# Retention and two MLP layers on one core: sums of the right operands on VectorE, weight preparation outside one block, a fourth w_out buffer

## Chip, cores and metric

The kernel runs on one core of a Trainium2 chip. The metric is the device time in microseconds, the median of three runs; a profiled execution of the same program stands beside them.

## What is computed

```python
# q, k, v: (4, 8, 576, 64); x is then (2304, 512); w_in (512, 2048), w_out (2048, 512), twice
scores = (q @ k.T) / sqrt(64) * gamma_h ** (i - j)   # for i >= j, else 0
x = (scores @ v), heads side by side                 # 2304 tokens x 512
h = x @ w_in;  x = (max(h, 0) ** 2) @ w_out          # layer one
h = x @ w_in2; out = (h * clip(h + 3, 0, 6) / 6) @ w_out2   # layer two
```

The weights arrive as 8-byte floats and all products are to have the accuracy of 4-byte floats. The kernel decodes the weights itself and splits each factor into a high part (what the matmul's input type holds) and a low part (the rest); a product is three matmuls: high by high, high by low, low by high.

## The kernel before

**Layer one** goes over five blocks of tokens (`FIRST`, line 26: 512, 512, 512, 256, 512) and in each over 16 chunks of the 2048 hidden columns. One chunk of one block is a unit; there are 80, numbered from 0, and the block of 256 is units 48 to 63. A unit i issues, in this order: the 12 matmuls of h (`emit_h`, line 348); in the last three units of a block the high and low parts of the next block's x (`split_x`); the parts of the w_in chunk of unit i + 1 (`split_in`, high on ScalarE, low on VectorE from unit 17 on); in units 1 to 16 the parts of a w_out chunk (`split_out`); relu on ScalarE, square, and the parts of g (`emit_g`); pieces of the retention of later tokens; the 12 matmuls of y for unit i - 2 (`y_steps`, `LAG` = 2); the load of the w_out parts of unit i + 1 (`load_out`); and preparation steps. The first block decodes layer one's weights as it goes and stores the w_out parts to memory (`keep`), from where later blocks load them. The w_out tiles rotate through the pool `wop` of three buffers; in units 15 and 16 the last two tiles made by `split_out` and the first reloads alternate in it.

**Preparation** (`ready_steps`, line 414) makes the weights of layer two: eight groups of 11 steps, in the order decode, decode, sums (GpSimd), split, decode, split, w_out split, split, decode, split, w_out split. A decode has two ScalarE and four VectorE operations and a load of the next staged weight; a split has its high part on ScalarE and its low part on GpSimd, a w_out split its low part on VectorE; each ends in a store. They stand at the end of units 16 to 73, `READY` (line 46), at 88/58 = 1.5 steps a unit, issued when a whole step is owed.

**Layer two** uses the seven products of a Strassen scheme (`PRODUCTS`, line 48: P1 P6 P2 P7 P5 P4 P3) on three blocks of 768 tokens (`SECOND`), two halves of 384 each. A pair (`pair`, line 533) is two chunks of hidden columns in one block: seven products of six matmuls, and between the products, in slots 0 to 6 (`between`), the y matmuls of the pair before and side work. There are 24 pairs, eight a block. The left operands come from memory (`load_left`), the right operands are made once a block from x by `operand_steps` (line 461): four sums on GpSimd (768 columns in one operation, line 468) and seven splits (`split_to`, lines 174 and 175: high part on ScalarE, low part on VectorE, 768 columns each). For the first block this is done in the last units of layer one and slots 0, 2 and 4 of the first pair; for a later block in slots 0, 2, 4 and 5 of the last pair of the block before and slots 0, 2 and 4 of its own first pair. Each operand lies in the place that the same product's operand of the block before had, so it can't be made before that is used up.

Each engine works its instructions in the order of the program, and the order is written by hand. The SP queue issues nearly all DMAs, also in order: a transfer that waits holds back those behind it.

Of the kernel before, what the change touches and what calls it, by code (L numbers as in the profile page):

```python
# [9 lines left out]
F32 = mybir.dt.float32  # L10
# [4 lines left out]
ALU = mybir.AluOpType  # L15
# [29 lines left out]

READY = (16, 74)

# [18 lines left out]
def retention_moe_moe2(ctx, tc, qk, qk_last, kv, w_in, w_out, w_in2, w_out2, consts, out):  # L66
# [16 lines left out]
    one = pool("one", 1)  # L83
    wop = pool("wo", 3)
    cp = pool("cp", 3)
    banks = pool("banks", 1, space=PSUM)
# [14 lines left out]
    def place(tag, shape, dtype, name):  # L101


        return one.tile(shape, dtype, tag=tag, name=name)
# [356 lines left out]
    def operand_steps(j):  # L461

        t0 = SECOND[j]
        b = lambda k, t: xall[:, 2 * k:2 * k + 2, t0 + HALF * t:t0 + HALF * t + HALF]
        tt = {}

        def minus(dst, x, y):
            nc.gpsimd.tensor_tensor(out=dst, in0=x, in1=y, op=ALU.subtract)  # L468

        def step(i):  # L470
            name = PRODUCTS[i]
            if name == "P6":
                tt[2] = place("ret", [128, 2, 512], F32, "t2")[:, :, :HALF]
                minus(tt[2], b(1, 1), b(0, 0))
            if name == "P7":
                minus(b(0, 1), b(1, 1), b(0, 1))
            src = {
                "P1": b(0, 0), "P6": tt.get(2), "P2": b(1, 0), "P7": b(0, 1), "P5": b(0, 0),
                "P4": b(1, 0), "P3": b(1, 1),
            }[name]  # L480
            if i < 3:
                t = place(f"x{i + 4}", [128, 2, 2, HALF], F32R, "xop")
            else:
                t = place(f"x{i - 3}", [128, 2, 2, HALF], F32R, "xop")
            split_to(t[:, 0], t[:, 1], src, nc.vector)
            operands[j, name] = t
            if name == "P1":
                minus(b(0, 0), b(0, 1), b(0, 0))
            if name == "P2":
                minus(b(1, 0), b(1, 0), tt[2])  # L490

        return [lambda i=i: step(i) for i in range(len(PRODUCTS))]

# [136 lines left out]
    with tc.manual_schedule():  # L630
# [39 lines left out]
        ready = [f for p in range(NPAIR) for f in ready_steps(p)]  # L670
        pace, owed = len(ready) / (READY[1] - READY[0]), 0
        following = operand_steps(0)
        for i, (pos, c) in enumerate(units):
# [55 lines left out]
        following.pop(0)()  # L729
        load_left(1)  # L730
# [5 lines left out]
        for k in range(total):  # L736
# [69 lines left out]
```

## Time and profile before

| | |
|---|---|
| median of 3 runs | 933.23 us (931.39 to 933.29) |
| profiled execution | 932.34 us, span 930.4 us |
| TensorE matmuls busy | 876.8 us (94%) |
| VectorE / ScalarE / GpSimd busy | 594.2 / 424.0 / 190.9 us |
| mean granted TensorE clock | 0.978 |
| mean memory traffic | 207 GB/s |

A busy share is an average over stages; what sets the time of one stage is read from the waits of TensorE in it. In the rows PE is TensorE's matmul, PEld its weight load, which runs ahead of the matmul, DVE is VectorE, ACT ScalarE, POOL GpSimd, SP SyncE (SPq its queue of DMA issues). L175 is line 175 of the kernel before.

### The profile page before, as it was taken

How to read it: one execution, taken by the hardware profiler on the slowest of the kernel's cores; microseconds unless marked ns; L12 is line 12 of the kernel's file. 1: busy time of each engine (PE TensorE's matmuls, PEld its weight loads, DVE VectorE, ACT ScalarE, POOL GpSimd, SP SyncE). 2: the span in 40 equal slices, each digit the busy share in tenths (PEclk: the TensorE clock that was granted, in tenths of full speed). 3: DMA queues.
4: the chain of work that ended last, by engine and by line, in shares of the span. 5: the costliest groups of instructions: out<-in, count | busy, mean ns of one | idle time of the engine just before them, and what ended most of it. 6: DMA issues, size and time to landing. Idle time of an engine off the chain costs nothing.

```text
span 930.4 us, 13279 instructions
## 1 busy us (share of the span) xinstructions
PE 876.8 (94%) x4986; PEld 743.5 (80%) x4986; DVE 594.2 (64%) x933; ACT 424.0 (46%) x777; POOL 190.9 (21%) x157
## 2 busy tenths in 40 slices
PE   8788989899999999987999999999799998999998
PEld 6666766677888888876888888898688896888896
DVE  5699987777686768878765653535644346544443
ACT  2466675534554355545553443334343333433332
POOL 4455533323122313242131200002100003000000
PEclk8899999899999999998999999999899999999999
DMA  9357776675676676977747554545175554375432
GB/s 351 112 182 254 226 258 210 210 260 206 198 238 223 223 260 218 312 247 273 248 134 235 217 190 156 210 163 205 67 294 194 179 186 164 114 279 195 171 124 90
DMA packets 72879, 192.56 MB, mean 207 GB/s; under 512 B 10480, under 2 KB 26864, under 8 KB 72816
## 3 DMA queue, kind: packets, MB, share of 16 engines
q1 hardware_dynamic: 72672, 191.39, 59.9%
q8 instruction: 39, 0.64, 0.3%
q10 hardware_dynamic: 144, 0.34, 0.1%
q14 instruction: 24, 0.20, 0.1%
HBM read 155.53 MB, written 36.18 MB: 206 GB/s over the span
## 4 chain that ended last, share of the span: by engine, by line
PE 69%; DVE 13%; ACT 8%; DMA 4%; issue 4%; POOL 1%; SPq 0%; DVEq 0%; ACTq 0%; POOLq 0%
PE yps L517 19%; PE hps L547 17%; PE yps L388 15%; PE hps L354 15%; DMA stage<-in_w_in_dram 4%; DVE a L154 2%; DVE a L163 2%; DVE wd L169 1%; ACT a L152 1%; DVE ret L238 1%; DVE a L157 1%; PE vps L277 1%; DVE xop L175 1%; DVE win L175 1%; ACT xop L174 1%
## 5 line engine op out<-in xcount | busy, mean ns | idle before, releaser
L354 PE MATMUL hps<-xring,win 128*128 128x512 f32 (+1 forms) x960 | 220.7, 377 | 24.9 <-DVE win L175 12.5
L517 PE MATMUL yps<-wo,g 128*128 128x512 f32 x864 | 228.7, 396 | 8.7 <-ACT g L560 4.7
L388 PE MATMUL yps<-g,wo 128*128 128x512 f32 (+1 forms) x960 | 218.1, 375 | 1.9 <-POOL wo L175 1.2
L354 PEld LDWEIGHTS hps<-xring,win 128*128 128x128 f32 x960 | 169.3, 192 | 62.6 <-DVE win L175 14.9
L547 PE MATMUL hps<-xop,win 128*128 128x384 f32 x1008 | 206.8, 339 | 2.9 <-DVE xop L175 1.7
L547 PEld LDWEIGHTS hps<-xop,win 128*128 128x128 f32 x1008 | 182.8, 190 | 20.0 <-DVE xop L175 2.4
L388 PEld LDWEIGHTS yps<-g,wo 128*128 128x128 f32 x960 | 169.3, 192 | 35.0 <-POOL wo L175 2.0
L517 PEld LDWEIGHTS yps<-wo,g 128*128 128x128 f32 x864 | 160.8, 189 | 33.6 <-ACT g L560 5.3
L174 ACT ACTIVATE g<-r 128x512 fp32r<-128x512 f32 (+1 forms) x80 | 47.2, 590 | 101.7 <-DVE r L371 101.1
L566 DVE TENSOR_TENSOR u<-hps,u 128x384 f32<-128x384 f32 x48 | 26.8, 557 | 96.1 <-PE hps L547 96.1
L175 DVE TENSOR_TENSOR g<-r,g 128x512 fp32r<-128x512 f32 (+1 forms) x80 | 57.0, 713 | 42.2 <-ACT g L174 40.7
L367 ACT ACTIVATE r<-hps 128x512 f32<-128x512 f32 (+1 forms) x80 | 44.0, 550 | 75.8 <-PE hps L354 75.7
L560 ACT ACTIVATE g<-c 128x384 fp32r<-128x384 f32 x72 | 37.8, 525 | 88.1 <-DVE c L559 86.6
L371 DVE TENSOR_TENSOR r<-r 128x512 f32<-128x512 f32 (+1 forms) x64 | 47.8, 747 | 34.1 <-ACT r L367 34.1
L468 POOL TENSOR_TENSOR xall<-xall 128x768 f32<-128x768 f32 x6 | 12.0, 2006 | 249.1 <-DVE xop L175 249.1
L558 ACT ACTIVATE v<-c,three 128x384 f32<-128x384 f32 x72 | 44.4, 617 | 38.8 <-DVE c L566 37.9
L175 DVE TENSOR_TENSOR win<-w,win 128x512 fp32r<-128x512 f32 x63 | 52.1, 827 | 3.2 <-ACT win L174 3.2
L154 DVE TENSOR_SCALAR a<-a 128x512 f32<-128x512 f32 x64 | 43.5, 680 | 15.1 <-ACT a L152 14.9
L559 DVE SCALAR_TENSOR_TENSOR c<-v,c 128x384 f32<-128x384 f32 x72 | 43.2, 600 | 12.9 <-ACT v L558 12.9
L174 ACT ACTIVATE win<-w 128x512 fp32r<-128x512 f32 x80 | 49.5, 619 | 0.0
L585 ACT ACTIVATE c<-hps 128x384 f32<-128x384 f32 x24 | 11.8, 492 | 82.7 <-PE hps L547 82.7
L152 ACT ACTIVATE a<-stage 128x512 f32<-128x512 f32 x64 | 42.2, 660 | 13.0 <-DMA stage<-in_w_in_dram 12.3
(75 smaller groups left out, 864.6 us busy)
## 6 DMA issues: line engine op xcount, KB each, us to landing
wo<-kept SPq DMA_DIRECT2D x112, 512.0 KB, 4.1
win<-kept SPq DMA_DIRECT2D x72, 512.0 KB, 4.4
kept<-ready SPq DMA_DIRECT2D x40, 512.0 KB, 5.0
stage<-in_w_in_dram SPq DMA_DIRECT2D x32, 512.0 KB, 4.7
stage<-in_w_out_dram SPq DMA_DIRECT2D x32, 512.0 KB, 5.2
kept<-wo SPq DMA_DIRECT2D x16, 512.0 KB, 6.6
qkt<-in_qk_dram SPq DMA_DIRECT2D x14, 512.0 KB, 5.9
kvt<-in_kv_dram SPq DMA_DIRECT2D x14, 512.0 KB, 6.7
```

What stands on the lines that cost most here:

```text
L152: nc.scalar.activation(out=a, in_=high.bitcast(F32), func=ACTF.Abs)
L154: nc.vector.tensor_scalar(out=a, in0=a, scalar1=LEAST, scalar2=MOST, op0=ALU.max, op1=ALU.min)
L174: nc.scalar.activation(out=hi, in_=src, func=ACTF.Copy)
L175: lo_engine.tensor_tensor(out=lo, in0=src, in1=hi.bitcast(F32), op=ALU.subtract)
L354: nc.tensor.matmul(out=h, lhsT=w[:, wp, kk * 128:kk * 128 + 128], rhs=xs[pos, kk][xp], start=m == 0, stop=m == 3 * KD - 1,)
L367: nc.scalar.activation(out=r, in_=h, func=ACTF.Relu)
L371: nc.vector.tensor_tensor(out=r, in0=r, in1=r, op=ALU.mult)
L388: nc.tensor.matmul(out=p, lhsT=w[:, wp, m * 128:m * 128 + 128], rhs=gt[:, gpart, :n], start=c == 0 and e == 0, stop=c == NCH - 1 and e == 2,)
L517: nc.tensor.matmul(out=p, lhsT=gt[m // 3][:, gpart, m % 3 * 128:][:, :128], rhs=w[:, wp], start=first and e == 0, stop=last and e == 2,)
L547: nc.tensor.matmul(out=to, lhsT=wl[k][:, half, wp, o], rhs=x[:, xp, f], start=first and m == 0, stop=last and m == 5, skip_group_check=True,)
L558: nc.scalar.activation(out=v, in_=c, func=ACTF.Relu, bias=three)
L559: nc.vector.scalar_tensor_tensor(out=c, in0=v, scalar=6.0, in1=c, op0=ALU.min, op1=ALU.mult)
```

## The change

- The preparation steps stand in units 17 to 47 and 64 to 74 (42 units, 88/42 = 2.1 steps a unit); the block of 256 has none.
- The pool of w_out tiles has four buffers instead of three, that of the activations `c` and `r` two instead of three.
- The four sums of the right operands, now called T1, T2, T4 and T3, are on VectorE, each in two halves of 384 columns. For a later block they stand in pairs 2 to 5 of the block before, slots 1 and 4; for the first block in units 75 to 78. T1 and T4 get tiles of their own in the pool of decoded weights.
- The high and low part of an operand are no longer made together. High parts are two ScalarE operations of 384 columns, low parts two VectorE operations. For a later block, the high parts of the first five products stand in slots 0, 1, 3, 4, 6 of the last pair of the block before, the low parts one slot later; the last two in slots 1 and 3, low parts in 2 and 4, of its first pair. For the first block high parts stand in units 76 to 78 and behind the loop.

```diff
-READY = (16, 74)
+READY = [u for u in range(17, 75) if u // 16 != 3]
-    wop = pool("wo", 3)
-    cp = pool("cp", 3)
+    wop = pool("wo", 4)
+    cp = pool("cp", 2)
 def operand_steps(j):
-        def minus(dst, x, y):
-            nc.gpsimd.tensor_tensor(out=dst, in0=x, in1=y, op=ALU.subtract)
-        def step(i):
...
-            split_to(t[:, 0], t[:, 1], src, nc.vector)
+        b = lambda k, t: [xall[:, 2 * k + f, t0 + HALF * t:t0 + HALF * t + HALF] for f in range(2)]
+        def minus(name, f):
+            x, y, kept_in = {
+                "T1": (b(0, 1), b(0, 0), None), "T2": (b(1, 1), src.get("T1"), "ret"),
+                "T4": (b(1, 0), src.get("T2"), None), "T3": (b(1, 1), b(0, 1), b(0, 1)),
+            }[name]
...
+            nc.vector.tensor_tensor(out=src[name][f], in0=x[f], in1=y[f], op=ALU.subtract)
+        def high(i):
+            t = place(f"x{(i + 4) % 7}", [128, 2, 2, HALF], F32R, "xop")
+            operands[j, PRODUCTS[i]] = t
+            for f in range(2):
+                nc.scalar.activation(out=t[:, 0, f], in_=of[PRODUCTS[i]]()[f], func=ACTF.Copy)
+        def low(i):
+            t = operands[j, PRODUCTS[i]]
+            for f in range(2):
+                nc.vector.tensor_tensor(
+                    out=t[:, 1, f], in0=of[PRODUCTS[i]]()[f], in1=t[:, 0, f].bitcast(F32), op=ALU.subtract
+                )
 layer one, end of unit i
-            if READY[0] <= i:
+            if i in READY:
                 owed += pace
-                while ready and owed >= 1:
+                while ready and owed >= 0.999:
-                if c in (NCH - 4, NCH - 3, NCH - 2):
-                    following.pop(0)()
+                if NCH - 5 <= c < NCH - 1:
+                    for f in sums[2 * (c - NCH + 5):][:2]:
+                        f()
+                if c >= NCH - 3:
+                    lows[c - NCH + 3]()
+                if NCH - 4 <= c < NCH - 1:
+                    highs[c - NCH + 4]()
 layer two, side work of pair p
-            if p == NPAIR - 1 and j + 1 < len(SECOND):
-                following = operand_steps(j + 1)
-                for i in (0, 2, 4, 5):
-                    side[i].append(following.pop(0))
-                for i in (0, 2, 4):
-                    side[i].append(following.pop(0))
+                if 2 <= p < 6:
+                    for i, f in zip((1, 4), sums[2 * (p - 2):][:2]):
+                        side[i].append(f)
+                if p == NPAIR - 1:
+                    highs, lows = highs2, lows2
+                    for i, at in enumerate((0, 1, 3, 4, 6)):
+                        if at < 6:
+                            side[at + 1].append(lows[i])
+                        side[at].append(highs[i])
+                for i, at in ((5, 1), (6, 3)):
+                    side[at].append(highs[i])
+                    side[at + 1].append(lows[i])
```

## Rows read from the trace of the kernel before

**Rows 1.** The page, busy us, share of span and count of each engine.
```profile
PE 876.8 (94%) x4986; PEld 743.5 (80%) x4986; DVE 594.2 (64%) x933; ACT 424.0 (46%) x777; POOL 190.9 (21%) x157
```

**Rows 2.** Windows: stretch, length, busy us (count) PE, PEld, DVE, ACT, POOL; clock; DMA.
```profile
186.00:360.00 174.00, 174.00 (x997) 140.49 (x996) 127.84 (x188) 84.02 (x152) 45.08 (x41) 1.00 0.70 233
360.00:448.00 88.00, 76.76 (x669) 69.03 (x667) 71.27 (x115) 45.77 (x98) 28.36 (x27) 0.96 0.78 256
...
429.00:436.00 7.00, 5.73 (x27) 5.73 (x28) 5.27 (x9) 3.73 (x8) 4.39 (x5) 0.52 0.48 166
```

**Rows 3.** Waits of weight loads, 359 to 449 us: total us, times, longest.
```profile
PEld hps L354 <- DVE win L175: 12.1, 8, 3.6
PEld hps L354 <- ACT win L174: 1.2, 1, 1.2
```

**Rows 4.** Timeline of weight loads, block of 256: start, us, instruction, count, [idle <-releaser].
```profile
422.28 1.51 PEld L354 LDWEIGHTS hps<-xring,win 128*128 128x128 f32 x12
...
430.27 2.21 PEld L354 LDWEIGHTS hps<-xring,win 128*128 128x128 f32 x10 [3.58 <-DVE win L175]
```

**Rows 5.** A group of VectorE, 359 to 449 us: count, busy us, mean ns, idle before.
```profile
L169 DVE CUSTOM_DVE_ANT_0 wd<-a,r 128x1024 uint16<-128x1024 uint16 x9 | 7.1, 789 | 1.3 <-DVE a L163 0.2 <-ACT r L153 0.2
```

**Rows 6.** Timeline of VectorE and weight loads, 262 to 271 us, units 31 to 33.
```profile
263.05 0.42 DVE L154 TENSOR_SCALAR a<-a 128x512 f32<-128x512 f32 x1
...
267.82 0.69 DVE L175 TENSOR_TENSOR win<-w,win 128x512 fp32r<-128x512 f32 x1
...
268.16 2.68 PEld L354 LDWEIGHTS hps<-xring,win 128*128 128x128 f32 x12
```

**Rows 7.** Timelines of SP, ScalarE and TensorE, 150 to 188 us; last, ScalarE's waits.
```profile
151.20 0.50 SPq L340 DMA_DIRECT2D kept<-wo  x1
...
157.48 0.42 SPq L340 DMA_DIRECT2D kept<-wo  x1
...
162.84 0.63 ACT L174 ACTIVATE wo<-wd 128x512 fp32r<-128x512 f32 x1 [6.54 <-PE hps L354]
...
152.40 0.73 PE L354 MATMUL hps<-xring,win 128*128 128x512 f32 x2 [0.48 <-ACT win L174]
...
170.74 4.63 PE L354 MATMUL hps<-xring,win 128*128 128x512 f32 x10 [2.28 <-DVE win L175]
...
186.71 2.88 PE L354 MATMUL hps<-xring,win 128*128 128x512 f32 x12
...
ACT wo L174 <- DMA kept<-wo: 7.0, 2, 3.7
```

**Rows 8.** Groups of the whole span: count, busy us, mean ns, idle before.
```profile
L562 DVE TENSOR_TENSOR g<-c,g 128x384 fp32r<-128x384 f32 x72 | 39.8, 552 | 12.8 <-ACT g L560 12.4
...
L175 DVE TENSOR_TENSOR xop<-xall,xop 128x768 fp32r<-128x768 f32 x18 | 17.3, 958 | 21.1 <-ACT xop L174 20.9
```

**Rows 9.** Timeline of layer two's first block change: pairs 7, 8 and 9.
```profile
635.53 1.12 PEld L547 LDWEIGHTS hps<-xop,win 128*128 128x128 f32 x6
...
651.21 1.12 PEld L547 LDWEIGHTS hps<-xop,win 128*128 128x128 f32 x6
651.84 2.13 POOL L468 TENSOR_TENSOR xall<-xall 128x768 f32<-128x768 f32 x1
652.22 2.16 DVE L559 SCALAR_TENSOR_TENSOR c<-v,c 128x384 f32<-128x384 f32 x1
...
654.99 0.29 PEld L517 LDWEIGHTS yps<-wo,g 128*128 128x128 f32 x1 [2.65 <-ACT g L560]
...
674.60 1.12 PEld L547 LDWEIGHTS hps<-xop,win 128*128 128x128 f32 x6
```

**Rows 10.** Timeline of weight loads at the end of pair 0.
```profile
536.72 0.19 PEld L547 LDWEIGHTS hps<-xop,win 128*128 128x128 f32 x1 [1.65 <-ACT xop L174]
537.71 0.82 PEld L547 LDWEIGHTS hps<-xop,win 128*128 128x128 f32 x5 [0.81 <-DVE xop L175]
538.52 2.32 PEld L388 LDWEIGHTS yps<-g,wo 128*128 128x128 f32 x6
```

More of the change, by code (lines that the diff above doesn't have):

```diff
@@ L492, in operand_steps @@
-        return [lambda i=i: step(i) for i in range(len(PRODUCTS))]
+        src = {}
+        b = lambda k, t: [xall[:, 2 * k + f, t0 + HALF * t:t0 + HALF * t + HALF] for f in range(2)]
[3 more added lines that the diff above has]
+                "T4": (b(1, 0), src.get("T2"), None), "T3": (b(1, 1), b(0, 1), b(0, 1)),
+            }[name]
+            if f == 0:
+                if kept_in is None:
+                    src[name] = [wdp.tile([128, 512], F32, tag="wd", name="t")[:, :HALF] for _ in range(2)]
+                elif kept_in == "ret":
+                    t = place("ret", [128, 2, 512], F32, "t2")
+                    src[name] = [t[:, e, :HALF] for e in range(2)]
+                else:
+                    src[name] = kept_in
+            nc.vector.tensor_tensor(out=src[name][f], in0=x[f], in1=y[f], op=ALU.subtract)
@@ new lines, in operand_steps @@
+        sums = [lambda name=name, f=f: minus(name, f) for name in ("T1", "T2", "T4", "T3") for f in range(2)]
+        of = {
+            "P1": lambda: b(0, 0), "P6": lambda: src["T2"], "P2": lambda: b(1, 0), "P7": lambda: src["T3"],
+            "P5": lambda: src["T1"], "P4": lambda: src["T4"], "P3": lambda: b(1, 1),
+        }
+        def high(i):
[3 more added lines that the diff above has]
+                nc.scalar.activation(out=t[:, 0, f], in_=of[PRODUCTS[i]]()[f], func=ACTF.Copy)
@@ L494, in load_left @@
+        def low(i):
[4 more added lines that the diff above has]
+                )
+        return sums, [lambda i=i: high(i) for i in range(7)], [lambda i=i: low(i) for i in range(7)]
     def load_left(k):
@@ L670, in retention_moe_moe2 @@
         ready = [f for p in range(NPAIR) for f in ready_steps(p)]
-        pace, owed = len(ready) / (READY[1] - READY[0]), 0
-        following = operand_steps(0)
+        pace, owed = len(ready) / len(READY), 0
+        sums, highs, lows = operand_steps(0)
         for i, (pos, c) in enumerate(units):
@@ L728, in retention_moe_moe2 @@
             pending += y_steps(*u)
-        following.pop(0)()
+        for i in (3, 4):
+            highs[i]()
+        for i in (3, 4):
+            lows[i]()
         load_left(1)
@@ L740, in retention_moe_moe2 @@
             side = [[] for _ in range(7)]
-            if p == NPAIR - 1 and j + 1 < len(SECOND):
-                following = operand_steps(j + 1)
-                for i in (0, 2, 4, 5):
-                    side[i].append(following.pop(0))
-            if p == 0:
-                for i in (0, 2, 4):
-                    side[i].append(following.pop(0))
+            if j + 1 < len(SECOND):
+                if p == 2:
+                    sums, highs2, lows2 = operand_steps(j + 1)
+                if 2 <= p < 6:
[7 more added lines that the diff above has]
+                        side[at].append(highs[i])
+            if p == 0:
+                if j:
+                    side[0].append(lows[4])
+                for i, at in ((5, 1), (6, 3)):
+                    side[at].append(highs[i])
+                    side[at + 1].append(lows[i])
             for i, e in ((4, 1), (6, 0)):
```

20 lines of the change are left out of this document (removed).

## The prediction

> **What bounds the kernel now.** I read the busy times first: TensorE's matmuls are busy 94% of the span, VectorE 64% [rows 1], so TensorE sets the time almost everywhere and what can be won is its waits. The windows by stage then say where these are. From 186 to 360 us TensorE is busy in all of its 174.00 us at the full clock; in the block of 256 and its two ends, 360 to 448 us, only in 76.76 of 88.00 [rows 2]. The table of waits for that stretch names the cause: 12.1 us in eight waits for "DVE win", the low part of the next w_in tile, and 1.2 us for its high part on ScalarE [rows 3]. The timeline shows the cost: twelve weight loads of a 256-wide group take 1.51 us with no wait, the worst group came after a wait of 3.58 us and then took 2.21 us for ten loads [rows 4], because the granted clock there was 0.52, the lower of its two levels (1.2 GHz), after TensorE had waited several times in the units before [rows 2]. Three other places lose time: units 16 to 19 at the end of the first block, and the three beginnings of a block of the second layer; they are below.
>
> **The block of 256.** A unit there needs two groups of 1.51 us [rows 4], about 3.0 us, and in that time VectorE has to do the tails of the activation, a low part, and 24 of the 88 preparation steps (one and a half a unit by the pace in the code). Among these are nine decodes [rows 5] and, by the code, four w_out splits with their low part on VectorE, 0.69 us for that shape [rows 6]. The price of a decode comes from a place where two run one after another: from 263.05 to the next operation at 267.82 us, 4.77 for two, 2.4 each [rows 6]. Removed from the block: 9 x 2.4 + 4 x 0.69 = 24.4 us of VectorE's 71.27 [rows 2]. The 47 us left stand beside some 72 of matmuls (88.0 less the 15.4 below), so VectorE stops being late. The waits of 13.3 us go, and with them the half clock: 2.21 - 10/12 x 1.51 = 0.95 us on that one group, about 2.1 with the next. Sum 15.4 us. What is late next: at the hand-over to the last block two parts of x, which can only be made once the last h group frees their slots, stand ahead of the w_in part on both engines, and units 64 and 65 now begin with a split and two decodes in groups of 4.2 us (their y is still 256 wide). I leave 1.4 us there. Term: **-14.0 us**, ends -9 and -16.
>
> **Where the steps go.** 88 steps now fall in 42 units instead of 58, 2.1 a unit: by the code's arithmetic 65 in units 17 to 47 (48 before) and 23 in 64 to 74 (16 before). For 186 to 360 us that is five decodes and three splits more, 5 x 2.4 + 3 x 0.69 = 14 us on VectorE, 127.84 + 14 = 142 of 174 us [rows 2], 82%. The mean fits, so the question is bunching. Two decodes now fall together in units 17, 33, 38 and 70. Before, that happened once in a 512 block, in unit 31: the decodes and the w_in part behind them ended just as the h group began at 268.16 us, and it began without a wait [rows 6]. So one such pair is just covered; where retention or the block's copies share the unit it would miss by about a microsecond. The stage loads and stores of these steps leave the SP queue with them and stand ahead of the w_out loads of the 512 blocks; those are issued two units ahead of their use, some 11 us, so I cost that at nothing, and a late load would be paid by a y group. Term: **+2 us**, ends 0 and +12 (twelve if each of some eight bunches costs a wait of 1.2 us and one starts the half clock).
>
> **The fourth w_out buffer.** With three, the sixteenth w_out tile of layer one takes the place of the fourteenth (the first reload stands between them), whose store SP issued at 157.48 us; ScalarE, in order, sat 6.54 us until 162.84 us [rows 7]. The row names a matmul as releaser, but the store's landing is what the code waits for. Behind that instruction stood the relu of unit 16, the decode of unit 16 and the w_in part of unit 18, and TensorE waited 2.28 us for that part at 170.74 and then ran at half clock (ten matmuls in 4.63 us). From h of unit 16 (152.40) to h of unit 20 (186.71) it took 34.3 us [rows 7]; eight groups of 2.7 us [rows 6] and about 3 us of retention are 24.6. With four buffers the tile waits for the store issued at 151.20 instead, that of the thirteenth, 6.3 us earlier [rows 7]. I take 6 of the 9.7 us, since unit 17 now has both decodes at once, which delays the part of unit 19: ends 2 and 9. The same wait occurs twice more in the first block, 7.0 us in sum [rows 7], where VectorE is the busier engine; 2.5 us there, ends 0 and 7. Term: **-8.5 us**. In the second layer the buffer moves loads forward that nobody waits for: nothing. One activation buffer fewer costs nothing, since each is read out within a unit and two remain.
>
> **The second layer.** A steady pair takes 15.68 us (635.53 to 651.21). The first pair of the next block takes 23.39 (651.21 to 674.60) [rows 9], 7.7 more, and the one after repeats it within 0.2 us. The cause is read on VectorE: an operation that otherwise takes 0.55 us [rows 8] takes 2.16 at 652.22, beside a GpSimd subtraction of 2.13 at 651.84, and TensorE's y group waits 2.65 us for the g that hangs on it [rows 9]. The change takes these twelve subtractions, 2.1 us like the one at 651.84 [rows 9], from GpSimd and puts 24 halves of 0.55 us [rows 8] on VectorE, two a pair in pairs 2 to 5 (for the first block in the last units of layer one); a part that was 0.958 [rows 8] becomes two of 0.55, +0.15 us on each of 21. VectorE's cost, 13 + 3 us, is spread over places where it is idle half the time and waits for the next product between its steps. High and low parts move one product apart and each is ready at least a product before its use. I looked for the tightest place: in the last pair the low part of P7 stands before the sum of P3, and the first y of the next pair needs a g part that comes behind that; adding the rows leaves it some 0.2 us. For the first block the same repair is made before the loop: now 1.65 + 0.81 us of waits and six loads in 2.32 us [rows 10] where half of 2.68 [rows 6] is normal, 3.4 us. Sum 2 x 7.7 + 3.4 = 18.8; I keep 0.8 for tight places. Term: **-18.0 us**, ends -12 and -19.
>
> **Sum.** -14.0 + 2 - 8.5 - 18.0 = -38.5. The profiled execution took 932.34 us (span 930.4), 0.9 below the median of 933.23; 932.34 - 38.5 = 893.8, which I call **893.5 us**.
>
> **Rivals.** (a) VectorE becomes the bound in the 512 blocks, not only bunched. Before, GpSimd is busy 45.08 us in 186 to 360, and with the moved steps about 15 us more of its splits and sums fall beside VectorE. The rows of the second layer show that an operation beside GpSimd can take almost four times as long [rows 9]. If the eight bunches each cost 1.2 us and three start the half clock (2.1 us each, as above), the 512 blocks lose about 16 instead of 2: 893.5 + 13 = 906. For it: the lengthened operations. Against it: the same stretch holds 45 us of GpSimd work already and has no wait. The Trainium skill bears on this rival (GPSIMD Engine Reference, Key points): GpSimd shares its memory interfaces with VectorE, and they contend where a VectorE instruction has two inputs in SBUF. By that rule the moved preparation makes VectorE dearer where it lands, and the time would be this rival's 906; the rows agree for two operations and show no wait in the 512 blocks.
> (b) The block changes of the second layer are only half mended: the high part of P5 stands on ScalarE ahead of the next pair's first copy, and the low parts ahead of g. If a wait of 2.5 us with a half clock stays at both, that is 5 each, 893.5 + 10 = 903. Against it: the lengthening by GpSimd, the larger half of the loss, cannot occur.
> (c) More comes back: the whole 9.7 us at unit 16 (3.7 more), all of the 7.0 in the first block (4.5 more), no new waits (2): 883.
> (d) The fourth buffer does not do what it is for, because the earlier store also lands late (SP issues stores behind loads that wait): the 8.5 us stay, 902.
> (e) Slower than before: VectorE's operations lengthen by 42% throughout the 512 blocks, beside more GpSimd work. Then 142 us become 202 in a stretch of 174: +28; the last block adds about 6, and half clock at four places 8: 893.5 + 42 = 935. It decides from the point where lengthening passes 174/142, 22%; beyond, each per cent is 1.4 us. Against it: the part of unit 33's group came in time after two decodes that were not lengthened at all [rows 6].
>
> **Chances.** Forecast 56%, (a) 17%, (b) 9%, (c) 12%, (d) 3%, (e) 3%. The range from 882 to 909 leaves out (e), the far end of (a) and the far end of (c), about 15%. A difference of 0.2% is about what a measurement of this kernel can tell from none. Faster by more than that 96%, within it 1%, slower 3%.
>
> **What would show it.** In the profile after: no GpSimd operation in the second layer, pairs 8 and 16 within 1 us of 15.7; the block of 256 with VectorE near half busy and no wait for win; ScalarE without a wait of 6 us before the sixteenth w_out tile; new waits for win, if any, two units behind units 17, 33, 38, 64, 65 and 70. The forecast is wrong if the 512 blocks show a wait in most units (a), if g is still waited for at a block change (b), or if the wait before the w_out tile stays (d).

## The result and the profile of the changed kernel

The changed kernel takes **902.45 us** in the median of four runs (901.15 to 903.96), the kernel before, run beside it, 932.59 (931.39 to 933.29): a ratio of 0.9679 with a 95% interval of 0.9656 to 0.9702. It is 30 us faster; the forecast was 893.5, with a range from 882 to 909. The profiled execution took 903.65 us (span 901.8), 28.7 less than the profiled one of before.

The page's first line, to be held against [rows 1]: TensorE's share rose from 94 to 96%, VectorE's from 64 to 67%, GpSimd's fell.

```profile
PE 869.3 (96%) x4986; PEld 739.3 (82%) x4986; DVE 601.5 (67%) x978; ACT 425.4 (47%) x798; POOL 169.4 (19%) x145
```

Stage by stage, in us between the starts of the weight loads of the h groups (for layer two of the first pair's):

| | to unit 0 | 0 to 16 | 16 to 20 | 20 to 48 | 48 to 66 | 66 to layer two | layer two |
|---|---|---|---|---|---|---|---|
| before | 38.1 | 114.3 | 34.1 | 173.3 | 88.7 | 76.1 | 405.8 |
| after | 39.2 | 116.1 | 25.7 | 180.0 | 72.7 | 80.9 | 387.3 |
| difference | +1.1 | +1.8 | -8.4 | +6.7 | -16.0 | +4.8 | -18.5 |

The windows of the changed kernel (columns as in [rows 2]) for units 20 to 48, for units 48 to 66 and for units 66 to 80, then two windows in the first block:

```profile
181.00:361.00 180.00, 174.91 (x993) 139.42 (x992) 149.60 (x212) 93.49 (x174) 58.37 (x52) 1.00 0.75 259
361.00:433.70 72.70, 72.49 (x674) 66.74 (x673) 43.55 (x80) 33.33 (x71) 8.98 (x8) 1.00 0.51 176
433.70:514.50 80.80, 77.58 (x338) 62.52 (x337) 62.31 (x92) 41.14 (x77) 18.38 (x16) 1.00 0.74 257
...
83.00:91.00 8.00, 6.96 (x18) 5.58 (x19) 7.90 (x14) 6.81 (x13) 3.66 (x3) 0.57 0.70 232
141.00:149.00 8.00, 7.41 (x20) 5.44 (x21) 7.80 (x9) 5.23 (x10) 4.25 (x3) 0.57 0.64 198
```

The block of 256 is now full: TensorE is busy in 72.49 of 72.70 us, where [rows 2] had 76.76 of 88.00, and VectorE works 43.55 us in it. The 512 blocks have paid for it. Their first stretch had no idle time [rows 2]; now five us are idle, at the full clock, with VectorE at 149.60 us. The table of waits of the weight loads for 181 to 515 us names what is waited for (total us, times, longest), and the second row, for 361 to 433.7 us alone, says that next to nothing of it lies in the block of 256:

```profile
PEld hps L354 <- DVE win L175: 13.1, 12, 2.3
```
```profile
PEld hps L354 <- DVE win L175: 0.4, 1, 0.4
```

It is the wait of [rows 3], in another place. How one of these twelve comes about is read from VectorE, GpSimd and the weight loads before unit 68 (start, us, engine, line):

```profile
444.48 0.95 DVE L154 TENSOR_SCALAR a<-a 128x512 f32<-128x512 f32 x1
445.46 1.40 DVE L157 TENSOR_SCALAR a<-a 128x512 int32<-128x512 int32 x1
446.90 0.69 DVE L163 SCALAR_TENSOR_TENSOR a<-stage,a 128x512 int32<-128x512 int32 x1
447.73 0.69 DVE L169 CUSTOM_DVE_ANT_0 wd<-a,r 128x1024 uint16<-128x1024 uint16 x1
448.33 0.68 DVE L175 TENSOR_TENSOR win<-w,win 128x512 fp32r<-128x512 f32 x1
```
```profile
443.95 1.19 POOL L433 TENSOR_TENSOR sums<-wd,sums 128x256 f32<-128x256 f32 x1
445.11 1.47 POOL L175 TENSOR_TENSOR ready<-wd,ready 128x512 fp32r<-128x512 f32 x1
```
```profile
449.07 2.14 PEld L354 LDWEIGHTS hps<-xring,win 128*128 128x128 f32 x10 [2.11 <-DVE win L175]
```

The part that TensorE waits for takes 0.68 us and is not slow itself. It stands in VectorE's queue behind a decode, and that decode's first two operations took 0.95 and 1.40 us beside GpSimd's sums and split. The first of them took 0.42 in [rows 6], the second 0.43 behind it, with no GpSimd work beside them.

### The profile page after: what moved, and what is told of

Same layout as the page of the kernel before. It is cut to its first block, busy times and chain, and to the rows that moved or that the text cites. A ratio compares the mean times of both kernels' runs of the same rounds, so it can differ in the third digit from the quotient of the medians.

```text
span 901.8 us, 13422 instructions
## 1 busy us (share of the span) xinstructions
PE 869.3 (96%) x4986; PEld 739.3 (82%) x4986; DVE 601.5 (67%) x978; ACT 425.4 (47%) x798; POOL 169.4 (19%) x145
## 4 chain that ended last, share of the span: by engine, by line
PE 66%; DVE 17%; ACT 6%; issue 5%; DMA 4%; POOL 1%; SPq 0%; DVEq 0%; ACTq 0%; POOLq 0%
PE yps L526 22%; PE hps L556 20%; PE hps L354 11%; PE yps L388 10%; DMA stage<-in_w_in_dram 3%; DVE a L163 3%; DVE a L154 2%; DVE win L175 2%; DVE wd L169 2%; DVE r L371 2%; DVE a L157 2%; DVE g L175 1%; ACT g L174 1%; DVE ret L238 1%; PE vps L277 1%
## 5 line engine op out<-in xcount | busy, mean ns | idle before, releaser
L354 PE MATMUL hps<-xring,win 128*128 128x512 f32 (+1 forms) x960 | 223.6, 381 | 16.2 <-DVE win L175 8.6
L526 PE MATMUL yps<-wo,g 128*128 128x512 f32 x864 | 226.3, 394 | 0.1
L354 PEld LDWEIGHTS hps<-xring,win 128*128 128x128 f32 x960 | 169.9, 193 | 55.3 <-DVE win L175 13.8
L388 PE MATMUL yps<-g,wo 128*128 128x512 f32 (+1 forms) x960 | 214.9, 372 | 0.0
L556 PE MATMUL hps<-xop,win 128*128 128x384 f32 x1008 | 203.3, 336 | 0.0
L556 PEld LDWEIGHTS hps<-xop,win 128*128 128x128 f32 x1008 | 180.7, 188 | 15.4
L567 ACT ACTIVATE v<-c,three 128x384 f32<-128x384 f32 x72 | 44.4, 617 | 32.7 <-DVE c L575 31.4
L154 DVE TENSOR_SCALAR a<-a 128x512 f32<-128x512 f32 x64 | 46.4, 725 | 14.8 <-ACT a L152 14.7
L152 ACT ACTIVATE a<-stage 128x512 f32<-128x512 f32 x64 | 42.3, 661 | 17.2 <-DMA stage<-in_w_in_dram 16.6
L568 DVE SCALAR_TENSOR_TENSOR c<-v,c 128x384 f32<-128x384 f32 x72 | 40.0, 555 | 13.4 <-ACT v L567 13.4
L163 DVE SCALAR_TENSOR_TENSOR a<-stage,a 128x512 int32<-128x512 int32 x64 | 47.9, 765 | 1.3
L571 DVE TENSOR_TENSOR g<-c,g 128x384 fp32r<-128x384 f32 x72 | 39.7, 552 | 12.5 <-ACT g L569 12.4
```

What stands on the lines that cost most here:

```text
L152: nc.scalar.activation(out=a, in_=high.bitcast(F32), func=ACTF.Abs)
L154: nc.vector.tensor_scalar(out=a, in0=a, scalar1=LEAST, scalar2=MOST, op0=ALU.max, op1=ALU.min)
L163: nc.vector.scalar_tensor_tensor(out=a.bitcast(I32), in0=high, scalar=-0x40000000, in1=a.bitcast(I32), op0=ALU.bitwise_and, op1=ALU.bitwis ...
L354: nc.tensor.matmul(out=h, lhsT=w[:, wp, kk * 128:kk * 128 + 128], rhs=xs[pos, kk][xp], start=m == 0, stop=m == 3 * KD - 1,)
L388: nc.tensor.matmul(out=p, lhsT=w[:, wp, m * 128:m * 128 + 128], rhs=gt[:, gpart, :n], start=c == 0 and e == 0, stop=c == NCH - 1 and e == 2,)
L526: nc.tensor.matmul(out=p, lhsT=gt[m // 3][:, gpart, m % 3 * 128:][:, :128], rhs=w[:, wp], start=first and e == 0, stop=last and e == 2,)
```

## The experiments

The stage times of all kernels that ran, in the columns of the table above, are the base of what follows:

| | to 0 | 0-16 | 16-20 | 20-48 | 48-66 | 66-80 | layer two | median, ratio to before |
|---|---|---|---|---|---|---|---|---|
| before | 38.1 | 114.3 | 34.1 | 173.3 | 88.7 | 76.1 | 405.8 | |
| after | 39.2 | 116.1 | 25.7 | 180.0 | 72.7 | 80.9 | 387.3 | 902.45, 0.9679 [0.9656, 0.9702] |
| e1_ready_old | 38.8 | 116.0 | 25.2 | 173.3 | 89.7 | 76.1 | 387.2 | 908.48, 0.974 [0.9721, 0.9758] |
| e2_wo3 | 39.2 | 113.0 | 31.4 | 179.9 | 72.6 | 80.4 | 387.5 | 907.89, 0.9737 [0.9714, 0.976] |
| e5_wo4_only | 38.2 | 115.1 | 25.2 | 173.3 | 90.5 | 76.1 | 405.6 | 925.76, 0.9931 [0.9915, 0.9946] |
| e3_operands_old | 39.3 | 112.5 | 26.9 | 179.8 | 72.6 | 80.9 | 404.5 | 919.51, 0.9859 [0.9837, 0.9881] |
| e3a_sums_gpsimd | 38.9 | 113.6 | 26.2 | 179.1 | 72.7 | 81.7 | 390.4 | 907.37, 0.9723 [0.9704, 0.9741] |
| e6_no_gpsimd | 38.0 | 113.3 | 26.9 | 177.2 | 72.2 | 80.3 | 387.1 | 897.29, 0.9627 [0.9609, 0.9644] |
| e4_win_first | 39.1 | 112.6 | 26.2 | 178.5 | 72.2 | 78.2 | 387.3 | 897.24, 0.9617 [0.9597, 0.9638] |
| e9_win_two_ahead | 38.9 | 115.6 | 25.2 | 175.9 | 75.8 | 78.0 | 387.3 | 898.78, 0.9637 [0.9621, 0.9652] |
| e10_win_two_ahead_ready_old | 38.9 | 115.8 | 25.2 | 173.3 | 88.0 | 76.1 | 387.0 | 906.56, 0.9721 [0.9693, 0.9749] |
| e11_spread | 38.9 | 114.6 | 26.2 | 174.2 | 78.8 | 76.1 | 387.4 | 899.48, 0.9642 [0.962, 0.9663] |
| e12_spread_order | 38.7 | 114.0 | 26.1 | 173.7 | 79.0 | 76.1 | 387.4 | 896.80, 0.9613 [0.9594, 0.9631] |
| e13_spread_order_end | 38.8 | 116.0 | 25.2 | 173.3 | 78.4 | 76.1 | 387.5 | 897.21, 0.9621 [0.9608, 0.9634] |

One column needs a warning. Except in e2, the program of units 0 to 15 is that of the changed kernel in every run from e1 down, and it still took anything from 112.5 to 116.1 us, with a granted clock of 1.00 in some executions and 0.93 in that of the changed kernel. So single stages are compared below, and a difference of totals under 3.6 us may be the first block's. By the granted clock of this stage, three executions with four buffers had no half clock there (e3, e4 and e6, 1.00) and nine had some (0.93 to 0.99); the two with three buffers (before and e2) had none.

**The preparation steps back in the block of 256.**

```diff
-READY = [u for u in range(17, 75) if u // 16 != 3]
+READY = list(range(16, 74))
```

> The changed kernel with one part undone: preparation steps in units 16 to 73 at 1.5 a unit again, the block of 256 included. Theory (queue order on VectorE): the block from h of unit 48 to h of unit 66 goes back from 72.7 to about 88 us, the waits for the w_in part that the changed kernel has in the 512 blocks (11.5 us longer from unit 20 to 48 and 66 to the second layer) go: 902.5 + 16 - 11.5 = about 907. Rival (the preparation costs the same wherever it stands, and the gain is all from the other two parts): 902 to 903.

908.48 us. The 512 blocks are back at 173.3 and 76.1, what they took before, and the block of 256 at 89.7, with the old wait (weight loads, 349 to 439 us):

```profile
PEld hps L354 <- DVE win L175: 12.2, 7, 3.6
```

This is the theory's 907 within 1.5 us. So the placement of the steps, and nothing else of the change, brings both the gain of 17.0 us there and the loss of 6.7 + 4.8 = 11.5 in the 512 blocks.

**Three w_out buffers again, and the fourth alone.** The first kernel undoes the buffers in the changed kernel, the second makes them alone in the kernel before (`wo` 4, `cp` 2). Both turn the two pools together, and `cp` has one buffer fewer where `wo` has one more; a pool that loses a buffer can't be what takes a wait away, so what is gained is put down to `wo`.

```diff
-    wop = pool("wo", 4)
-    cp = pool("cp", 2)
+    wop = pool("wo", 3)
+    cp = pool("cp", 3)
```

> The changed kernel with three w_out buffers and three activation buffers again. Theory: ScalarE waits about 6 us for a store's landing before the sixteenth w_out tile again, units 16 to 20 take about 34 instead of 25.7 us, and the first block is unchanged, since its three half-clock stretches are chance: 902.5 + 8 = about 910. Rival (the fourth buffer itself made the first block 3 us longer): units 0 to 16 take 114 instead of 116 us and the sum is about 907. Second rival (units 16 to 20 were mended by the later start of the preparation, not by the buffer): 900 to 903.

> The kernel before with only the buffers changed (four w_out, two activation). From the run with three (units 16 to 20 in 31.4 us beside 25.7) the fourth buffer is worth 5.7 us there. Theory: the same here, 34.1 to about 28, and nothing elsewhere: 932.5 - 6 = 926 to 927. Rival (it only pays together with the later start of the preparation): 931 to 932.5.

907.89 and 925.76. The rows of ScalarE for the sixteenth w_out tile, first with three buffers (e2), then with four (the changed kernel), then with four alone (e5); the wait of 6.54 us in [rows 7] is the one to hold them against:

```profile
162.54 0.63 ACT L174 ACTIVATE wo<-wd 128x512 fp32r<-128x512 f32 x1 [6.47 <-PE hps L354]
```
```profile
159.36 0.63 ACT L174 ACTIVATE wo<-wd 128x512 fp32r<-128x512 f32 x1 [1.96 <-DVE wd L169]
```
```profile
157.24 0.63 ACT L174 ACTIVATE wo<-wd 128x512 fp32r<-128x512 f32 x1 [1.96 <-DVE wd L169]
```

With three buffers the wait stays and names a matmul; with four it goes, and what ends the rest is the decode that the tile is split from. No matmul was changed, so the releaser in the row of before was not what held it, the buffer was. The times alone could not tell: in the kernel before, the store issued at 157.48 landed at 162.74, the h group that the row names ended at 162.75, and ScalarE went on at 162.84; in e2 the same store landed at 162.44, 0.1 us before ScalarE went on. The stage fell from 34.1 to 25.2 with the buffer alone. Undone in the changed kernel it rises only to 31.4; there the decode of unit 16 no longer stands behind the waiting instruction (the steps begin in unit 17), which may be why, but no run tried this by itself. The rival that the buffer made the first block longer is open: e2's first block took 113.0 us, that of e3, e4 and e6, with four buffers, 112.5 to 113.3, but these three are the ones without half clock.

**Layer two as before, and then only its sums.** The first kernel is the kernel before with the new placement of the steps and the new buffers, and with the old operands and side work:

```diff
-READY = (16, 74)
+READY = [u for u in range(17, 75) if u // 16 != 3]
...
-    wop = pool("wo", 3)
-    cp = pool("cp", 3)
+    wop = pool("wo", 4)
+    cp = pool("cp", 2)
...
```

> The changed kernel with the right operands made as before: sums on GpSimd in the last and first pairs of a block, high and low parts together. Theory: the second layer goes back from 387.3 to 405.8 us, the rest stays: 902.5 + 18.6 = 921. Rival (part of that gain came from the earlier end of layer one or from the fourth buffer): 910 to 917.

919.51 us, 17 above the changed kernel, and layer two takes 17.2 more (404.5 against 387.3). Its block change shows the waits of before; under them the same place in the changed kernel, where P1 of pairs 8 and 9 begins:

```profile
640.78 0.29 PEld L517 LDWEIGHTS yps<-wo,g 128*128 128x128 f32 x1 [2.66 <-ACT g L560]
643.44 0.50 PEld L517 LDWEIGHTS yps<-wo,g 128*128 128x128 f32 x2 [2.37 <-DVE g L562]
644.04 2.04 PEld L547 LDWEIGHTS hps<-xop,win 128*128 128x128 f32 x6
```
```profile
637.57 1.12 PEld L556 LDWEIGHTS hps<-xop,win 128*128 128x128 f32 x6
...
653.25 1.12 PEld L556 LDWEIGHTS hps<-xop,win 128*128 128x128 f32 x6
```

653.25 - 637.57 = 15.68, a steady pair, for 23.39 in [rows 9]; pair 16, the next block change, takes 15.69 for 23.24, and the first pair 13.01 for 16.38. The clock granted in layer two is 1.00 where it was 0.98.

The second kernel leaves the new order of the parts and gives the sums back to GpSimd:

```diff
-            nc.vector.tensor_tensor(out=src[name][f], in0=x[f], in1=y[f], op=ALU.subtract)
+            nc.gpsimd.tensor_tensor(out=src[name][f], in0=x[f], in1=y[f], op=ALU.subtract)
```

> The changed kernel with only the engine of the four sums of the right operands changed back: they stay in halves of 384, in pairs 2 to 5 and units 75 to 78, but run on GpSimd. Theory (what cost 7.7 us at each block change was where the sums stood, beside the chain that ends in g): VectorE's operations in these pairs lengthen but nobody waits, total 902 to 903, second layer 387 to 388. Rival (GpSimd beside VectorE costs wherever it stands): one wait of some 0.5 to 1 us in each of pairs 2 to 5, 10 and more in sum, 908 to 912.

907.37 us in the median; its profiled execution took 904.39, and layer two 3.1 us more than in the changed kernel. Neither of the two outcomes expected came: something is lost, but not in pairs 2 to 5. The sums did not run in the pairs in which they are issued. GpSimd has nothing else to do there, so it took them as soon as their tiles came free: those of the second block from 515.03 us on, in pair 0, those of the third from 640.41 on, in pair 8. Only those places lost time: pair 0 takes 15.14 us for 13.01, pairs 8 and 9 16.13 and 16.44 for 15.69 each; pairs 2 to 7 take 15.69 as in the changed kernel. In pair 0 one sees how. VectorE and GpSimd with the sums on GpSimd, and the weight load that waited:

```profile
517.54 4.57 POOL L480 TENSOR_TENSOR t<-xall,t 128x384 f32<-128x384 f32 x4
522.08 2.60 POOL L480 TENSOR_TENSOR xall<-xall 128x384 f32<-128x384 f32 x2
```
```profile
521.13 1.40 DVE L571 TENSOR_TENSOR g<-c,g 128x384 fp32r<-128x384 f32 x1
522.45 1.36 DVE L568 SCALAR_TENSOR_TENSOR u<-v,u 128x384 f32<-128x384 f32 x1
523.74 1.82 DVE L497 TENSOR_TENSOR xop<-xall,xop 128x384 fp32r<-128x384 f32 x2
```
```profile
525.14 0.82 PEld L556 LDWEIGHTS hps<-xop,win 128*128 128x128 f32 x5 [2.27 <-DVE xop L497]
```

The same three in the changed kernel, with no GpSimd work beside them:

```profile
523.53 0.55 DVE L571 TENSOR_TENSOR g<-c,g 128x384 fp32r<-128x384 f32 x1
524.30 0.56 DVE L568 SCALAR_TENSOR_TENSOR u<-v,u 128x384 f32<-128x384 f32 x1 [0.23 <-ACT v L567]
524.78 1.02 DVE L497 TENSOR_TENSOR xop<-xall,xop 128x384 fp32r<-128x384 f32 x2
```

So the lengthening is real and costs a wait where a part is needed at once. But with the new order it is worth 0.44 + 0.75 = 1.2 us in pairs 8 and 9, where the loss was 7.7; most of the gain comes from what e3a keeps, the new order and places of the sums and parts and their halves. These were not taken apart, and sums on VectorE in the old places were not tried.

**Why the 512 blocks lost time: no GpSimd work.** This kernel leaves out the four sums of the left operands and their low parts; plain copies on ScalarE stand in their place.

```diff
-            op(out=half(s1, 0), in0=half(b, 0), in1=half(b, 1), op=ALU.add)
...
+            nc.scalar.activation(out=s1, in_=b, func=ACTF.Copy)
+            nc.scalar.activation(out=s0, in_=a, func=ACTF.Copy)
...
```

> The changed kernel with the GpSimd work of the weight preparation (sums and low parts of the splits) replaced by plain copies of the same size on ScalarE; so the sums and low parts of layer two's w_in are left out of the computation. The order on VectorE is the same. Theory (order alone): waits for the w_in part in units 20 to 48 and 66 to 80 stay near 13 us, total 901 to 903. Rival (the operations lengthened beside GpSimd make the difference between covered and late): VectorE's busy time in units 20 to 48 falls from 149.6 to about 135 us, the waits to a third, total 893 to 896.

The window of units 20 to 48 and the waits from 178 to 515 us:

```profile
178.20:355.40 177.20, 174.81 (x994) 139.47 (x993) 129.16 (x212) 108.25 (x204) 11.96 (x12) 1.00 0.77 265
```
```profile
PEld hps L354 <- DVE win L175: 6.1, 7, 1.7
PEld hps L354 <- ACT win L174: 3.1, 2, 1.9
```

The same 212 operations of VectorE take 129.16 us and not 149.60: 20 us of its time in this stretch are lengthening beside GpSimd. The wait before unit 68, 2.11 us above, is 0.63 here. Yet the two 512 stretches give back only 2.8 + 0.6 of their 11.5 us, and 6.1 us of waits for VectorE's part remain, about half and not a third; another 3.1 are for ScalarE, which has the added copies. So lengthening is a part of the loss. That it is not the whole this run does not show cleanly, since the copies also hold VectorE up: in units 20 to 48 it waits 6.6 us for ScalarE at the first operation of a decode, where the changed kernel has 2.9, and 4.1 us for the high part of w_in, where it has 0.3.

**Why the 512 blocks lost time: the place in the queue.** In e4 the w_in parts of unit i + 2 are issued at the end of unit i, from unit 16 on, ahead of the preparation steps; in e9 at the beginning of unit i, behind its h group. Everything else is as in the changed kernel. The edit of e4 (in e9 the added lines stand right behind the first ones):

```diff
-            if i + 1 < len(units):
+            if i <= NCH:
                 split_in(*units[i + 1], nc.gpsimd if pos == 0 else nc.vector)
...
+            if NCH <= i < len(units) - 2:
+                split_in(*units[i + 2], nc.vector)
             if i in READY:
```

> The changed kernel with one thing moved: from unit 18 on the parts of the w_in chunk are issued at the end of the unit two before, ahead of the preparation steps, not at the start of the unit before, behind them. No work is added. Theory (queue order: the low part is late because it stands behind decodes on VectorE): nearly all waits for it in the 512 blocks go, 11.5 us there becomes 1 to 2, total 891 to 893. Rival (VectorE's operations beside GpSimd are so much longer that it is the bound there): the wait turns up at the next thing VectorE makes, the low part of g, and the total stays at 899 to 903.

> The changed kernel with one thing moved: from unit 16 on the parts of the w_in chunk of unit i + 2 are issued at the start of unit i, right behind its h matmuls, so that a whole unit lies between them and their use. In the run that put them at the end of unit i (e4_win_first) they waited behind the retention mask and the low part of g instead, and 4 us were left. Theory (only the order in VectorE's queue makes the part late): waits for it in units 20 to 80 fall from 13 us to about 1, units 20 to 48 take 173 to 175 and 66 to 80 about 76 us, total 890 to 892. Rival (VectorE beside GpSimd is the bound of these units): something else VectorE makes is waited for, total 896 to 898 as before.

897.24 and 898.78, in neither case the total of the theory. In e4 the waits for that part fall from 13.8 to 3.5 us (150 to 520 us; first fence), in e9 they are gone; what is late in e9 instead shows in its waits from 179.7 to 515 us (second fence):

```profile
PEld hps L354 <- DVE win L175: 3.5, 4, 2.0
```
```profile
PEld yps L388 <- DVE xall L395: 1.8, 2, 1.5
PEld yps L388 <- ACT xall L397: 1.8, 1, 1.8
...
PEld hps L354 <- DVE ret L238: 1.3, 1, 1.3
...
PEld hps L354 <- ACT xring L174: 1.0, 1, 1.0
```

The copies of y, the mask of the retention and the parts of x stand behind the same decodes. The 512 stretches gain 1.5 + 2.7 in e4 and 4.1 + 2.9 in e9, and e9 gives 3.1 back in the block of 256. VectorE's queue is worked in order, and e9 has the same work in it (147.12 us busy in units 20 to 48 for 149.60): with the bunches left as they are, both runs are still late for something, and the order chooses for what.

**Could the order alone have mended the block of 256?** e9 with the steps where they were:

```diff
-READY = [u for u in range(17, 75) if u // 16 != 3]
+READY = list(range(16, 74))
```

> The w_in parts two units ahead (as in e9_win_two_ahead) with the preparation in units 16 to 73 again, the block of 256 included: is the move of the preparation still needed once the order is mended? Theory (in the block of 256 VectorE has 71 to 72 us of work for 72 us of matmuls, so no order mends it): units 48 to 66 take 80 to 84 us, 20 to 48 and 66 to 80 are at 173 and 76, total 899 to 903. Rival (only the order made that block slow too): 74 to 75 us there, total 891 to 893.

```profile
353.50:441.50 88.00, 77.95 (x674) 70.08 (x673) 71.19 (x117) 45.49 (x98) 29.23 (x27) 0.96 0.76 261
```

No: 906.56 us, and the block takes 88.0 us, as before (88.7). Fewer of the waits there are now for the part (weight loads, 353 to 442 us), and the parts of the next block's x are late as well:

```profile
PEld hps L354 <- DVE win L175: 5.8, 3, 3.6
PEld hps L354 <- DVE xring L175: 2.5, 1, 2.5
```

VectorE's 71.19 us stand beside some 72 us of matmuls. That no order at all would fit them in is the theory and is not shown; two places of the part were tried, that of e1 and this one.

**The steps thinner, and in another order.** e11 is e9 with a few steps in the block of 256 and none in the first and last unit of a block; e12 also changes the order in a group, so that no two decodes follow one another (but in the first group); e13 is e12 without steps in the last units of the block of 256.

```diff
+READY = [u for u in range(17, 75) if u % 16 not in (0, 15) and (u // 16 != 3 or u % 2)]
```
```diff
...
-            lambda: dec(c, 0), lambda: dec(c + 1, 0), sums,
-            lambda: split(0), lambda: dec(c, 1), lambda: split(1), lambda: out_split(c),
-            lambda: split(2), lambda: dec(c + 1, 1), lambda: split(3), lambda: out_split(c + 1),
+            lambda: dec(c, 0), *behind, lambda: dec(c + 1, 0), sums,
+            lambda: dec(c, 1), lambda: split(0), lambda: split(1),
+            lambda: dec(c + 1, 1), lambda: out_split(c), lambda: split(2), lambda: split(3), *ahead,
```
```diff
+READY = [u for u in range(17, 75) if u % 16 not in (0, 15) and (u // 16 != 3 or u % 2 and u < 59)]
```

> The w_in parts two units ahead, and the preparation spread by VectorE's free time: 45 units, every second unit of the block of 256, and in the 512 blocks not the first and last unit of a block, where the copies of y and the parts of x stand. Theory (what is left in e9_win_two_ahead, about 6 us, is the copies and the x parts late behind decodes): units 20 to 48 about 174, 48 to 66 73 to 74, 66 to 80 76 to 77, total 892 to 895. Rival (VectorE's mean load beside GpSimd is the limit): 897 to 900.

> As e11_spread, with the eleven steps of a group reordered so that no two decodes are neighbours (a w_out split, the sums and splits between them). Theory (bunches of two decodes are the rest of the lateness): 1 to 2 us less than e11_spread, 890 to 894. Rival (bunching no longer matters with a unit of lead): the same as e11_spread within 1 us.

> As e12_spread_order, without preparation in units 59 and 61 (43 units). In e12 the 512 blocks are at their floor (173.7 and 76.1 us) and 6 us were lost at the end of the block of 256, where a decode stood ahead of the next block's x parts and w_in part. Theory (order again): units 48 to 66 take 73 to 74 us, the 512 blocks lose at most 1 by the denser pace, total 890 to 893. Rival (the loss there comes from the x parts themselves, with one w_in part less lead in short units): 78 to 79 us there, total 896 to 898.

899.48, 896.80 and 897.21: each total is above its theory, e11's and e13's are where the rivals put them. The 512 blocks are back at 173.3 to 174.2 and 76.1, with VectorE at 134.5 to 137.5 us in units 20 to 48. So these blocks can hold a good part of the moved work without a loss. But the rest stands in the block of 256 again, which takes 78.4 to 79.0 for 72.7. From unit 20 to layer two the three take 327.8 to 329.1 us, e4 and e9 328.9 and 329.7, the changed kernel 333.6: some 4 to 6 of its 11.5 us come back, and no run shows that the rest can. The new order of the steps alone is worth little: e12 is 0.5 us below e11 in units 20 to 48, 0.2 above it in the block of 256, and equal in units 66 to 80. In e12 the end of the block of 256 loses time, in e13 its beginning; weight loads, first e12, then e13:

```profile
420.20 1.36 PEld L354 LDWEIGHTS hps<-xring,win 128*128 128x128 f32 x4 [2.38 <-DVE win L175]
```
```profile
356.65 0.19 PEld L354 LDWEIGHTS hps<-xring,win 128*128 128x128 f32 x1 [2.48 <-ACT xring L174]
358.75 0.60 PEld L354 LDWEIGHTS hps<-xring,win 128*128 128x128 f32 x3 [1.91 <-DVE xring L175]
```

Both are places where the parts of the next block's x, which need slots that the last h group frees, meet other work in the queue, and behind both the clock fell to half for a while (the granted clock of e12 from 418 to 425 us is 0.65, that of e13 from 356 to 366 us 0.83). e13 came out where its rival had put it, for another cause: it mended the end and lost the beginning. The three, e4 and e9 beat the changed kernel by 3 to 6 us, the best (e12, e13 and e4) by 5.7, 5.2 and 5.2; the interval of e11 overlaps with that of the changed kernel. e13 does so with the same long first block as the changed kernel (116.0). The stages at about their best in these runs (113, 25.2, 173.3, 72.2, 76.1, 387, with 39.2 ahead of unit 0) would add up to a span of 886 for 901.8, but no run had them together, and 173.3 and 76.1 were not seen beside 72.2.

## Why the prediction was right, and where it was not

The sum was -38.5 and -28.7 came, inside the range. The mechanisms of the three gains held in the main; two terms were mis-sized by 15 us together, and 5 of these were made good by gains that came out larger than said, which is luck. Term by term:

- **The block of 256: -14.0 said (-9 to -16), -16.0 found.** The cause is shown by e1, and the working held: 47 us of VectorE forecast, 43.55 found, no wait left but 0.4 us. What was late next at the hand-over had been put at 1.4 us; the 0.4 us lie in unit 49, two units behind the steps of unit 47, and none at the hand-over. The bunch in units 64 and 65 that I named cost the following stage 1.9 and 0.4 us, in units 66 and 67.
- **The fourth buffer at units 16 to 20: -6 said (-2 to -9), -8.4 found**, -8.9 alone (e5). Mechanism as said; the two decodes in unit 17, for which I kept a third of it back, cost one wait of 0.6 us, in unit 19. The read of the profile that carried it, a releaser passed over for what the code waits for, is shown by e2 and e5.
- **The first block: -2.5 said, +2.9 found**, of which 1.1 lie ahead of unit 0, where nothing was changed. The two ScalarE waits of 7.0 us [rows 7] did go. Behind them ScalarE waits longer for the decodes (DVE wd: 25.1 us where it was 19.8), so VectorE sets the pace there, as the prediction feared when it took 2.5 of 7.0. At the full clock the block takes 112.5 to 113.3 us with four buffers (e3, e4, e6) and 113.0 and 114.3 with three (e2, before), so the gain is at most small. The profiled execution of the changed kernel lost more than that to stretches at half clock (two windows with a granted clock of 0.57 are shown above), of which e3 and e4, the same program there, had none. So the program does not always have them; whether the fourth buffer makes them likelier (nine executions of twelve with it, none of two without) and what starts them stays open.
- **The 512 blocks: +2 said (0 to +12), +11.5 found. This is the step that failed.** Two things in it were mis-sized, the price and the bunches. The decode was priced at 2.4 us from [rows 6], a place with no GpSimd work beside it. In units 20 to 48 of the changed kernel the four operations of a decode take 0.689 + 0.496 + 0.766 + 0.769 = 2.72 in the mean and the low part of a w_out split 0.97 for 0.69, and the window has 149.60 us of VectorE for 142 forecast. The sum priced only the five decodes and three splits that were added; the sixteen and eight already there became dearer too, from 2.49 and 0.73 in the same units of the kernel before. These are the groups (count, busy us, mean ns, idle before):

```profile
L169 DVE CUSTOM_DVE_ANT_0 wd<-a,r 128x1024 uint16<-128x1024 uint16 x21 | 16.2, 769 | 3.1 <-DVE a L163 1.3 <-ACT r L367 0.2 <-ACT r L153 0.2
L163 DVE SCALAR_TENSOR_TENSOR a<-stage,a 128x512 int32<-128x512 int32 x21 | 16.1, 766 | 0.7
L154 DVE TENSOR_SCALAR a<-a 128x512 f32<-128x512 f32 x21 | 14.5, 689 | 3.0 <-ACT a L152 2.9
L175 DVE TENSOR_TENSOR ready<-wd,ready 128x512 fp32r<-128x512 f32 x11 | 10.7, 973 | 2.2 <-ACT ready L174 1.9
L157 DVE TENSOR_SCALAR a<-a 128x512 int32<-128x512 int32 x21 | 10.4, 496 | 0.7
```

  The bunches: I had looked for two decodes in one unit, by rows where such a pair was just covered. Here it is not covered: two units behind every place that I named there is a wait, 0.6 us in unit 19 (ahead of the window of the twelve) and 2.0, 0.5, 1.9, 0.4 and 0.3 us in units 35, 40, 66, 67 and 72. The other seven of the twelve, in units 31, 33, 42, 47, 49, 68 and 76, 8.0 us together, I had not named. Before units 31, 47 and 68 the code has one decode in each of three or four neighbouring units (26 to 29, 42 to 45, 64 to 66); that this alone makes a bunch is not shown, since units 21 to 24 have it too and no wait follows. The mean of the twelve waits, 1.1 us, is close to the 1.2 with which the bound was worked out: there were more of them than the value counted, and none started the half clock. (Two slips of the working change little: the code puts 64 steps in units 17 to 47 and 24 in 64 to 74, not 65 and 23, and in rival (a) 16 instead of 2 is 14 more, 907.5.) That the lateness is one of place and bunches and not of VectorE as a whole is shown in part. e9, with the same work there, loses 4.5 us in place of 11.5. e11 to e13 lose at most 0.9, but with a part of the steps back in the block of 256.
- **Layer two: -18.0 said (-12 to -19), -18.5 found**; by e3, 17.2 of it are the operands' doing. The first pair gave 3.4 us and the two block changes 7.7 and 7.6, as the sum had them. The tight place in the last pair, which I had left at 0.2 us, held. One reason stays unproven: that lengthening beside GpSimd was the larger half of the loss in the old order was not tried; in the new order it is worth 1.2 us at a block change (e3a).

Of the rivals, (a) comes nearest: there are new waits in the 512 blocks, and they lost 11.5 of the some 16 us that it gave, but without the half clock that it counted in these stages: the windows show 1.00, so its loss is all waits, and not in most units. The waits of 2.5 us at the block changes in (b) are not in the trace, (d) is refuted by e5, (e) by the stage itself, and of (c) the gain at unit 16 came almost whole (8.4 of 9.7) while the rest did not. The rule of the Trainium skill weighed against the trace (GPSIMD Engine Reference, Key points) holds for operations with two inputs: they shorten where GpSimd's work goes (e6, the low part of w_in from 882 to 717 ns) and lengthen where it comes (e3a). A second page of the Trainium skill puts it more sharply (SBUF — State Buffer, section "SBUF: two separate sides"): the loser of the shared ports is blocked for the other's whole instruction. The 0.55 that became 1.40 in pair 0 beside GpSimd operations of 1.1 to 1.3 us each, and the 2.16 in [rows 9] beside one of 2.13, agree with that roughly.

## What to carry to other kernels

Work taken out of a stage with no room for it must be counted again where it lands, at the price that it has there (beside the other engine's work), and unit by unit: a share of 82% of a stage says nothing of the units in which the work bunches. Where an in-order queue is late, issuing the late instruction earlier moves a part of the lateness to the next one behind the bunch (e4, e9); making the bunch smaller removed it there and paid elsewhere (e11 to e13). A releaser in a trace that has nothing to do with the tile that an instruction writes is a sign of a buffer; two things can end in the same 0.1 us, and one more buffer tells which it was.

## What was not expected of the hardware

VectorE's operation of line 154, which has one input and so is not covered by the condition of two that the prediction drew on, is lengthened the most beside GpSimd: 689 ns in the mean against 442 in e6 without the preparation's GpSimd work, 56% more, where the two-input low part of w_in went from 717 to 882, 23%. The clock of the first block differs between executions of the same instructions, a granted 0.93 to 1.00 and 112.5 to 116.1 us, as much as most of the later steps above are worth. And an idle GpSimd runs what is issued late in the program as soon as its tiles are free: in e3a the sums written into pairs 2 to 5 ran from 515.03 us, in pair 0, and those of the next block from 640.41 us, in pair 8.
